# Silu on ScalarE in two of six blocks, weight pieces converted in pairs, and second-MoE units in paired buffers

## The chip, the cores and the metric

The kernel runs on one core of one Trainium2 chip. The metric is the device time of one execution in microseconds (us); lower is better. The core has five engines that run side by side, each through its own list of instructions in a fixed order: TensorE (PE, matmul), VectorE (DVE), ScalarE (ACT), GpSimd (POOL) and SyncE (SP), which issues the DMAs. An instruction that waits holds up all that stands behind it on its engine.

## The reference, cut to what matters

Three stages follow each other: a chunked linear attention (a scan with state), a gated MoE layer with Silu, and a second layer with a softmax-weighted activation and a layer norm.

```python
def reference(...):
    attn_out = _attn_ref(x, a, B, C)                 # 4 x 8 heads x 768 x 32, state 16, chunks of 32
    x = attn_out.transpose(0, 2, 1, 3).reshape(3072, 256)
    rms = np.sqrt(np.mean(x * x, axis=-1, keepdims=True) + 1e-06)
    xn = x / rms * rms_g                             # first MoE: 256 -> 1536 -> 256
    g = xn @ w_gate
    silu = g * (1.0 / (1.0 + np.exp(-g)))
    x = silu * (xn @ w_val) @ w_out
    h = x @ w_in                                     # second MoE: 256 -> 1024 -> 256
    e = np.exp(h - h.max(-1, keepdims=True))
    solu = h * (e / (e.sum(-1, keepdims=True) + 1e-09))
    mu, var = solu.mean(-1, keepdims=True), solu.var(-1, keepdims=True)
    return ((solu - mu) / np.sqrt(var + 1e-06) * g_ln) @ w_out2
```

## The kernel before

The 3072 tokens are 24 units of 128, and four units make a block (`BLOCKS`), so there are 6 blocks. For a unit, an attention step `y(u)` is made on PE from the decay matrix L (tile `L`, exponentials on ACT, mask on POOL), the products B by C (`cb`, tile `pcb`, turned into L by the two DVE operations `mt`), and the state (`s2`, `sbd`). The result is squared (`sq`), summed on PE (`ms`), raised to -0.5 on POOL (`ts`, `pw`), spread by a transpose (`rb`), multiplied in (`xc`, `xn`) and split into a high and a low float part (`xh`, `xl`). Every large product is made as three matmuls in fp32r: high by high, low by high, high by low.

For a block, the first MoE runs over 12 slices f of 128 hidden columns: gate `gm` into `pg` (6 matmuls of 128x512), value `vm` into `pv` (6), and, two slices later, the output `o` (6) into `po`. Between them stand `th` (ACT, tanh), `si` and `mu` (DVE, Silu and the product with the value), `ah` (ACT) and `al` (DVE or POOL), the split of the product. `pg` and `pv` have one PSUM bank each, so the next `gm` waits until the last reader of `pg` is done. The second MoE runs by unit: `h` into `ph`, maximum, `ex`, `so`, sums, `va`, two transposes `t` with split, `f` and the store.

The weights come as 64-bit numbers in 26 pieces of 512 KB. Each is loaded (`w_load`), turned into fp32 by three integer operations on DVE (`w_conv`, tile `wt`), and split by ACT (`wh`) and DVE or POOL (`w`).

No engine list is written by hand. `plan()` holds for every step its engine, a duration, a due time, what it comes after and which buffers it takes; it walks through time, picks on each engine the ready step with the earliest due time, and writes the steps out in that order. Constants at the top (`PRO`, `FIRST`, `Y0`, `HLAG`, `WGAP` and others) set the due times. Units 0 to 3 are made ahead of the first block (the prologue); the units of block b+1 are made during block b.

## Time and profile before

| | us |
|---|---|
| median of 3 runs (lowest to highest) | 565.83 (565.73 to 566.2) |
| the profiled execution, its own time | 565.08 |
| span of its profile | 563.4 |
| PE, DVE, ACT, POOL busy in the span | 546.5, 390.9, 290.3, 84.8 |
| mean granted TensorE clock | 0.981 of 2.4 GHz |

Times in a trace are us from the start of the span. The own time is 1.7 us above the span and 0.75 us below the median; a change of the span is taken one for one into the median. "Busy" of PE counts a pipelined matmul to its modelled end, so what a matmul costs in a row of them is the distance between starts.

### The profile page before, as it was taken

The page shows a single profiled execution, that of the slowest core. Times are in us where ns is not written, and L with a number is a line of the kernel's source. Part 1 is how long each engine was busy: PE and PEld are TensorE (multiplying, and loading weights), DVE is VectorE, ACT ScalarE, POOL GpSimd, SP SyncE. Part 2 cuts the span into 40 slices and gives each one's busy share as a digit, 9 for nine tenths or more (in the row PEclk, how much of TensorE's full clock was granted, in tenths as well). Part 3 has the DMA queues.
Part 4 walks back from the last instruction along what each step waited for, and adds up shares of the span by engine and source line. Part 5 has one row for each costly group of instructions (what it writes and reads, how often), then busy time and mean ns, then how long its engine had stood idle before and what let it go on. Part 6 is the DMA issues. An engine that isn't in the chain of part 4 may idle for free.

```text
span 563.4 us, 9443 instructions
## 1 busy us (share of the span) xinstructions
PE 546.5 (97%) x3544; PEld 461.1 (82%) x3544; DVE 390.9 (69%) x789; ACT 290.3 (52%) x654; POOL 84.8 (15%) x118
## 2 busy tenths in 40 slices
PE   9879998899999999999999999999999999999996
PEld 8757886687888888888888888888888888888795
DVE  5788999999876776575684574684674574564763
ACT  6437654666555564463474454554543353343464
POOL 2333323212221010110111100110100000000010
PEclk9579999999999999999999999999999999999999
DMA  7464765542022021121120220220200000000000
GB/s 213 132 212 140 216 203 194 182 145 71 14 72 76 2 80 47 43 72 36 54 76 11 75 70 10 80 70 10 72 2 9 10 1 9 11 1 10 9 20 30
DMA packets 44366, 39.33 MB, mean 70 GB/s; under 512 B 3936, under 2 KB 36896, under 8 KB 44320
## 3 DMA queue, kind: packets, MB, share of 16 engines
q1 hardware_dynamic: 44320, 38.72, 22.5%
q8 instruction: 28, 0.46, 0.4%
q14 instruction: 18, 0.15, 0.1%
HBM read 35.37 MB, written 3.34 MB: 69 GB/s over the span
## 4 chain that ended last, share of the span: by engine, by line
PE 81%; DVE 15%; DMA 2%; issue 1%; ACT 1%; SPq 0%; POOL 0%; DVEq 0%; ACTq 0%; POOLq 0%
PE pv L558 15%; PE pg L558 15%; PE po L600 14%; PE ph L436 12%; PE pf L538 12%; PE pt L514 4%; PE pcb L301 3%; DVE wt L119 2%; PE y L326 2%; DVE wt L122 2%; DVE th L580 2%; PE y L321 1%; DVE al L592 1%; DVE th L576 1%; DVE L L307 1%; DVE wt L116 1%
## 5 line engine op out<-in xcount | busy, mean ns | idle before, releaser
L586 ACT ACTIVATE ah<-th 128x512 fp32r<-128x512 f32 x72 | 45.2, 628 | 52.2 <-PE po L600 38.8
L580 DVE TENSOR_TENSOR th<-pv,th 128x512 f32<-128x512 f32 x72 | 49.8, 691 | 29.2 <-PE pv L558 24.1
L592 DVE TENSOR_TENSOR al<-th,ah 128x512 fp32r<-128x512 f32 x70 | 49.3, 704 | 26.0 <-ACT ah L586 25.6
L576 DVE SCALAR_TENSOR_TENSOR th<-th,pg 128x512 f32<-128x512 f32 x72 | 49.1, 682 | 20.0 <-ACT th L572 19.7
L558 PE MATMUL pg<-xh,wg_h 128*128 128x512 f32 x144 | 59.5, 413 | 2.3 <-ACT xh L401 1.2
L600 PE MATMUL po<-ah,wo_h 128*128 128x512 f32 x144 | 60.3, 419 | 0.0
L600 PE MATMUL po<-al,wo_h 128*128 128x512 f32 x144 | 56.7, 394 | 2.3 <-DVE al L592 2.3
L558 PE MATMUL pv<-xh,wv_h 128*128 128x512 f32 x144 | 58.4, 406 | 0.0
L558 PE MATMUL pg<-xh,wg_l 128*128 128x512 f32 x144 | 57.0, 396 | 0.0
L558 PE MATMUL pg<-xl,wg_h 128*128 128x512 f32 x144 | 56.8, 394 | 0.0
L600 PE MATMUL po<-ah,wo_l 128*128 128x512 f32 x144 | 56.7, 394 | 0.0
L558 PE MATMUL pv<-xl,wv_h 128*128 128x512 f32 x144 | 56.5, 392 | 0.0
L558 PE MATMUL pv<-xh,wv_l 128*128 128x512 f32 x144 | 56.4, 392 | 0.0
L572 ACT ACTIVATE th<-pg 128x512 f32<-128x512 f32 x72 | 42.6, 592 | 26.6 <-PE pg L558 26.4
L502 POOL TENSOR_TENSOR sc<-sc,mhalf 128x1 f32<-128x1 f32 x24 | 14.1, 587 | 263.6 <-DVE sc L497 263.6
L237 ACT ACTIVATE L<-L,cneg 128x128 f32<-128x128 f32 x160 | 50.5, 390 | 0.6 <-DMA L<-crow 0.6
L460 ACT ACTIVATE ut<-ph,sc 128x1024 f32<-128x1024 f32 x20 | 22.3, 1116 | 54.5 <-DVE sc L447 54.5
L538 PE MATMUL pf<-wo_h,uth 128*128 128x256 f32 x176 | 49.6, 282 | 0.3 <-DVE utl L528 0.2
L538 PE MATMUL pf<-wo_h,utl 128*128 128x256 f32 x176 | 49.6, 282 | 0.0
L538 PE MATMUL pf<-wo_l,uth 128*128 128x256 f32 x176 | 49.5, 281 | 0.0
L447 DVE TENSOR_REDUCE sc<-ph 128x1 f32<-128x1024 f32 x20 | 24.5, 1225 | 31.7 <-PE ph L436 31.7
L523 ACT ACTIVATE uth<-pt 128x512 fp32r<-128x512 f32 x44 | 26.0, 595 | 31.1 <-PE pt L514 30.9
(138 smaller groups left out, 1225.2 us busy)
## 6 DMA issues: line engine op xcount, KB each, us to landing
L<-crow SPq DMA_DIRECT2D x20, 512.0 KB
stage<-in_wo_dram SPq DMA_DIRECT2D x10, 512.0 KB
xb<-in_xbt_dram SPq DMA_DIRECT2D x24, 192.0 KB
stage<-in_wg_dram SPq DMA_DIRECT2D x6, 512.0 KB
bc<-in_bcT_dram SPq DMA_DIRECT2D x48, 64.0 KB
stage<-in_wv_dram SPq DMA_DIRECT2D x6, 512.0 KB
out_dram<-ob SPq DMA_DIRECT2D x24, 128.0 KB
stage<-in_wi_dram SPq DMA_DIRECT2D x4, 512.0 KB
```

The source lines that it names most:

```text
L237: A.activation(d["L"][:, h], d["L"][:, h], AF.Exp, bias=cneg[:, u * 8 + h:u * 8 + h + 1])
L436: T.matmul(ph[c], xx[:, kk, k * P:(k + 1) * P], ww[:, kk, 512 * c:512 * c + 512], start=(i == 0), stop=(i == 5))
L447: V.tensor_reduce(out=sc[:, 0:1], in_=ph[0], axis=AX.X, op=ALU.max, negate=True)
L523: A.activation(d["uT"][0][:, 4 * c:4 * c + 4].rearrange("p k t -> p (k t)"), d["ptc", c], AF.Copy)
L538: T.matmul(d["pf"][:, 0:DM], uu[:, k], ww[:, k], start=(k == 0 and i == 0), stop=(k == 7 and i == 2))
L558: T.matmul(ps[:, :n], ww[:, kk, f * P:(f + 1) * P], xx[:, kk, :n], start=(i == 0), stop=(i == 5))
L572: A.activation(d["th"], d["pg"], AF.Tanh, scale=0.5)
L576: V.scalar_tensor_tensor(out=d["th"], in0=d["th"], scalar=1.0, in1=d["pg"], op0=ALU.add, op1=ALU.mult)
L580: V.tensor_tensor(out=d["th"], in0=d["pv"], in1=d["th"], op=ALU.mult)
L586: A.activation(d["ah"], d["th"], AF.Copy)
L592: e.tensor_tensor(out=d["al"], in0=d["th"], in1=d["ah"].bitcast(F32), op=ALU.subtract)
L600: T.matmul(po[b, m][:, :n], ww[:, f, m * P:(m + 1) * P], aa, start=(f == 0 and i == 0), stop=(f == NF - 1 and i == 2))
```

## The change

1. **Silu in blocks 0 and 1** (`SILU = 2`). ACT computes Silu at once into `th`; `si` falls away, and `mu` becomes one `scalar_tensor_tensor` with a factor of 2 (blocks 2 to 5 keep tanh, `si` and `mu`). Silu and Exp are not in one table set, so ACT loads a table wherever it goes from one to the other: 20 loads in the program where there were 2.
2. **Weight pieces in pairs.** Two pieces share one staging tile, and the three integer operations run over 1024 elements, 13 times, where they ran over 512, 26 times. A conversion starts when both loads of the pair have landed. There are 2 paired staging buffers (4 single ones before) and 2 paired `wt` tiles (3 single ones before).
3. **Second-MoE units share buffers in pairs**: units 2k and 2k+1 have the two halves of one tile of tag `u`.
4. **The factor `rgt` moves from `xn` to `xc`**: `xc` is two ACT operations of 128 elements, `xn` one DVE operation of 256.
5. **Planner**: other due times, the identity matrix is loaded a few places later, `nid` is not made, a table switch is priced, and small matmuls (`warm`) are put into planned PE gaps of the prologue (5 of them come out).

```diff
-PRO = 34.0
-FIRST = 63.0
+PRO = 31.0
+FIRST = 70.0
...
-Y0 = (9.0, 4.0)
-YPOS, YSPAN = 0.65, 1.0
+Y0 = (8.0, 4.5)
+YPOS, YSPAN = 0.55, 0.92
...
-EARLY = (-1.0, 1.5, 4.0, 6.0)
+EARLY = (-5.0, 2.0, 6.0, 9.0)
...
-HLAG = (50.0, 26.0)
+WOFF = -4.0
+HLAG = (70.0, 10.0, 1)
...
+SILU = 2
+TABLE = 1.3
...
     def w_conv(i, c):
-        v = stg[i].rearrange("p (f w) -> p f w", w=2)
+        v = stg[i, 2].rearrange("p s (f w) -> p (s f) w", w=2)
         if c == 0:
-            wtm[i] = sp.tile([P, 512], I32, name="wt", tag="wt", bufs=BUFS["wt"])
-        t = wtm[i]
+            wtm[i, 2] = sp.tile([P, 1024], I32, name="wt", tag="wt", bufs=BUFS["wt"])
+            for q in range(2):
+                wtm[i + q] = wtm[i, 2][:, 512 * q:512 * q + 512]
+        t = wtm[i, 2]
...
     def at_xc(u):
...
-        A.activation(d["xts"], d["y"][:, 0:256].rearrange("p (g i) -> p g i", g=2), AF.Copy)
+        for g in range(2):
+            A.activation(d["xts"][:, g], d["y"][:, g * P:(g + 1) * P], AF.Copy, scale=rgt[:, g:g + 1])
...
     def at_xn(u):
...
-        for g in range(2):
-            V.scalar_tensor_tensor(out=d["xts"][:, g], in0=d["xts"][:, g], scalar=rgt[:, g:g + 1],
-                                   in1=d["y"][:, 384:512], op0=ALU.mult, op1=ALU.mult)
+        V.tensor_tensor(out=d["xts"], in0=d["xts"], in1=d["y"][:, 384:512].unsqueeze(1).to_broadcast([P, 2, P]), op=ALU.mult)
...
         if c == 0:
-            d["u"] = sp.tile([P, FF2], F32, name="ut", tag="u", bufs=BUFS["u"])
+            if u % 2 == 0:
+                upair[0] = sp.tile([P, 2, FF2], F32, name="ut", tag="u", bufs=BUFS["u"])
+            d["u"] = upair[0][:, u % 2]
...
-        A.activation(d["th"], d["pg"], AF.Tanh, scale=0.5)
+        if b < SILU:
+            A.activation(d["th"], d["pg"], AF.Silu)
+        else:
+            A.activation(d["th"], d["pg"], AF.Tanh, scale=0.5)
...
-        V.tensor_tensor(out=d["th"], in0=d["pv"], in1=d["th"], op=ALU.mult)
+        if b < SILU:
+            V.scalar_tensor_tensor(out=d["th"], in0=d["th"], scalar=2.0, in1=d["pv"], op0=ALU.mult, op1=ALU.mult)
+        else:
+            V.tensor_tensor(out=d["th"], in0=d["pv"], in1=d["th"], op=ALU.mult)
...
+    def warm(u, n):
+        if u not in st:
+            return
+        for _ in range(n):
+            T.matmul(st[u]["y"][:, 322:384], ones, ones[:, 0:62], start=True, stop=True, skip_group_check=True)
...
+            if e == "ACT" and o.get("tab", table[0]) != table[0]:
+                t += TABLE
```

**PE in the prologue.** From the first `y` (rows `y<-L,xb` and `y<-xb`; `y<-cd` is its part with the state) to the second. `pcb` is `cb`, `y<-ones,sq` is `ms`, `pg` and `pv` from `um,la` are the exponents of L for a later unit, `y<-ident,r` is `rb`. Before:

```order
L301 MATMUL pcb<-bc 128x128 x8
L326 MATMUL y<-L,xb 32x128 x8
L331 MATMUL y<-xb 32x64 x4
L259 MATMUL pg<-um,la 128x128 x4
L361 MATMUL y<-ones,sq 128x1 x2
L259 MATMUL pv<-um,la 128x128 x4
L321 MATMUL y<-cd,sbd 128x128 x2
```

With the change:

```order
L338 MATMUL y<-L,xb 32x128 x8
L343 MATMUL y<-xb 32x64 x4
L313 MATMUL pcb<-bc 128x128 x8
L373 MATMUL y<-ones,sq 128x1 x2
L271 MATMUL pg<-um,la 128x128 x4
L271 MATMUL pv<-um,la 128x128 x4
L395 MATMUL y<-ident,r 128x128
L333 MATMUL y<-cd,sbd 128x128 x2
```

The `cb` of unit 1 now stands behind the first `y`, and the `ms` of unit 0 stands ahead of both groups of exponents instead of between them.

**DVE at the start of block 0.** The last conversions of the prologue and the first slices of the MoE (`th<-th,pg` is `si`, `th<-pv,th` or `th<-th,pv` is `mu`, `al` the low part). Before:

```order
L394 SCALAR_TENSOR_TENSOR xts<-xts,rgt,y 128x128 x2
L133 TENSOR_TENSOR wv_l<-wt,wv_h 128x2x256
L405 TENSOR_TENSOR xl<-xts,xh 128x2x128
L122 SCALAR_TENSOR_TENSOR wt<-stage,wt 128x512
L116 TENSOR_SCALAR wt<-stage 128x512
L119 SCALAR_TENSOR_TENSOR wt<-stage,wt 128x512
L133 TENSOR_TENSOR wo_l<-wt,wo_h 128x512
L122 SCALAR_TENSOR_TENSOR wt<-stage,wt 128x512
L576 SCALAR_TENSOR_TENSOR th<-th,pg 128x512
L580 TENSOR_TENSOR th<-pv,th 128x512
```

With the change, from the second half of the last `y` of the prologue on:

```order
L416 TENSOR_TENSOR xl<-xts,xh 128x2x128
L354 SCALAR_TENSOR_TENSOR s_461<-s_390,e_170,y 128x64
L360 TENSOR_TENSOR sbd<-cst,s_461 128x256
L386 TENSOR_SCALAR r<-y 128x1
L134 SCALAR_TENSOR_TENSOR wt<-stage,wt 128x1024
L406 TENSOR_TENSOR xts<-xts,y 128x256
L128 TENSOR_SCALAR wt<-stage 128x1024
L416 TENSOR_TENSOR xl<-xts,xh 128x2x128
L131 SCALAR_TENSOR_TENSOR wt<-stage,wt 128x1024
L145 TENSOR_TENSOR wo_l<-wt,wo_h 128x512
L145 TENSOR_TENSOR wg_l<-wt,wg_h 128x2x256
L134 SCALAR_TENSOR_TENSOR wt<-stage,wt 128x1024
```

The conversions are half as many and twice as long, and the last `xn` of the prologue (`xts`) stands behind one of 1024 elements.

**ACT in block 0.** From the second Tanh or Silu on (`th`); `L` with `x8` or `x4` are the exponentials of a unit of the next block, `w.._h` is the high part of a weight piece. Before:

```order
L572 ACTIVATE th<-pg 128x512
L237 ACTIVATE L<-L,cneg 128x128 x8
L246 ACTIVATE e_515<-e_515 128x128
L586 ACTIVATE ah<-th 128x512
L572 ACTIVATE th<-pg 128x512
L129 ACTIVATE wv_h<-wt 128x2x256
L237 ACTIVATE L<-L,cneg 128x128 x8
L586 ACTIVATE ah<-th 128x512
```

With the change:

```order
L587 ACTIVATE th<-pg 128x512
L141 ACTIVATE wv_h<-wt 128x2x256
L141 ACTIVATE wo_h<-wt 128x512
L606 ACTIVATE ah<-th 128x512
L587 ACTIVATE th<-pg 128x512
L249 ACT_TABLE_LOAD
L249 ACTIVATE L<-L,cneg 128x128 x8
L258 ACTIVATE e_494<-e_494 128x128
L606 ACTIVATE ah<-th 128x512
L249 ACTIVATE L<-L,cneg 128x128 x4
L141 ACTIVATE wg_h<-wt 128x2x256
```

The exponentials are one slice later, with a table load ahead of them; another load follows them, before the next Silu.

## Rows read from the trace of the kernel before

**Rows 1.** The page, busy time by engine (share of the span, instructions).

```profile
PE 546.5 (97%) x3544; PEld 461.1 (82%) x3544; DVE 390.9 (69%) x789; ACT 290.3 (52%) x654; POOL 84.8 (15%) x118
```

**Rows 2.** Windows: stretch, its length, busy time of each engine, granted clock, DMA, GB/s.

```profile
1.00:40.20 39.20, 33.11 (x286) 29.73 (x286) 26.97 (x65) 19.26 (x54) 13.27 (x18) 0.79 0.63 182
40.20:43.80 3.60, 3.58 (x8) 2.76 (x9) 3.26 (x7) 1.22 (x3) 0.00 (x0) 0.50 1.10 340
43.80:126.60 82.80, 79.38 (x520) 63.45 (x519) 80.17 (x150) 51.41 (x129) 24.60 (x28) 1.00 0.56 178
126.60:140.00 13.40, 12.43 (x88) 9.56 (x87) 12.95 (x23) 8.63 (x21) 3.13 (x4) 1.00 0.26 75
140.00:524.10 384.10, 384.10 (x2414) 325.03 (x2412) 244.37 (x482) 188.45 (x406) 40.63 (x60) 1.00 0.13 38
524.10:563.36 39.26, 33.93 (x233) 30.53 (x232) 23.22 (x67) 21.13 (x46) 2.75 (x5) 0.99 0.06 21
```

**Rows 3.** Timeline of PE in the prologue: start, duration, what, idle before.

```profile
11.76 1.16 PE L301 MATMUL pcb<-bc 16*128 16x128 f32 x16
12.85 0.64 PE L326 MATMUL y<-L,xb 128*32 128x128 f32 x16
...
13.54 1.16 PE L259 MATMUL pg<-um,la 128*128 128x128 f32 x8
...
16.64 1.01 PE L361 MATMUL y<-ones,sq 128*128 128x1 f32 x4 [1.95 <-DVE s L340]
...
19.36 1.06 PE L321 MATMUL y<-cd,sbd 128*128 128x128 f32 x4
...
28.42 1.06 PE L321 MATMUL y<-cd,sbd 128*128 128x128 f32 x4
...
33.23 0.61 PE L321 MATMUL y<-cd,sbd 128*128 128x128 f32 x4
...
40.22 0.79 PE L558 MATMUL pg<-xh,wg_h 128*128 128x512 f32 x1 [1.21 <-ACT xh L401]
```

**Rows 4.** Windows, PE alone: stretch, length, busy, granted clock, DMA, GB/s.

```profile
16.00:17.00 1.00, 0.36 (x2) 0.82 0.67 120
...
18.00:30.00 12.00, 12.00 (x89) 0.50 0.28 88
```

**Rows 5.** Groups of DVE by line: form, count, busy, mean ns, idle before; 43.8 to 126.6.

```profile
L119 DVE SCALAR_TENSOR_TENSOR wt<-stage,wt 128x512 int32<-128x512 int32 x16 | 12.0, 753 | 0.1
L122 DVE SCALAR_TENSOR_TENSOR wt<-stage,wt 128x512 int32<-128x512 int32 x16 | 11.9, 745 | 0.3
...
L576 DVE SCALAR_TENSOR_TENSOR th<-th,pg 128x512 f32<-128x512 f32 x16 | 10.9, 681 | 0.6 <-ACT th L572 0.6
...
L116 DVE TENSOR_SCALAR wt<-stage 128x512 int32<-128x512 int32 x17 | 7.9, 466 | 0.0
...
L394 DVE SCALAR_TENSOR_TENSOR xts<-xts,rgt,y 128x128 f32<-128x128 f32 x10 | 3.0, 341 | 0.0
```

**Rows 6.** Groups by line over the whole span, the nearest forms to the new operations.

```profile
L470 DVE SCALAR_TENSOR_TENSOR ut<-ph,ut 128x1024 f32<-128x1024 f32 x20 | 24.5, 1224 | 20.3 <-ACT ut L460 20.3
...
L405 DVE TENSOR_TENSOR xl<-xts,xh 128x256 fp32r<-128x256 f32 x24 | 10.4, 435 | 2.9 <-ACT xh L401 2.8
```

**Rows 7.** Timeline of ACT, the second of the two table loads.

```profile
5.53 1.28 ACT L267 ACT_TABLE_LOAD   x1 [2.06 <-DVE cneg L1026]
6.83 1.14 ACT L267 ACTIVATE L<-pg,cneg 128x128 f32<-128x128 f32 x4
```

**Rows 8.** Timeline of PE, 92 to 141, the rows with idle time before them.

```profile
95.75 0.50 PE L600 MATMUL po<-al,wo_h 128*128 128x512 f32 x1 [1.84 <-DVE al L592]
...
106.72 0.50 PE L600 MATMUL po<-al,wo_h 128*128 128x512 f32 x1 [0.49 <-DVE al L592]
...
111.87 0.50 PE L558 MATMUL pg<-xh,wg_h 128*128 128x512 f32 x1 [0.98 <-DVE th L576]
...
139.64 0.32 PE L383 MATMUL y<-ident,r 128*128 128x128 f32 x1 [0.78 <-POOL r L379]
```

More of the change, by code (lines that the diff above doesn't have):

```diff
@@ L407, in at_xl @@
         st.pop(u)
+    upair = [None]
     x2 = {}
@@ L799, in m_f4 @@
             m_f(u, c)
-    win = [f"{p}{i}" for i in range(18, 22) for p in ("wh", "w")] + ["wc25.2"]
+    win = [f"{p}{i}" for i in range(18, 22) for p in ("wh", "w")] + ["wc12.2"]
     wout = ["plo0", "plo1"]
@@ L901, in fused_kernel, with ld_ident, c_nid @@
     op("wd", "ACT", 0.35, 5.5, (c_wdec,), after=["sf"], use=["pd"])
+    def ld_ident():
+        S.dma_start(ident, consts[:, 3 * P:4 * P])
+    def c_nid():
+        V.tensor_scalar(out=nid, in0=ident, scalar1=-1.0, scalar2=None, op0=ALU.mult)
+    op("idn", "SP", 0.45, 4, (ld_ident,), kb=64)
+    if VIA_PE:
+        op("nid", "DVE", 0.25, 6, (c_nid,), after=["idn"])
+        for i in VIA_PE:
+            ops[f"wp{i}"]["after"].append("nid")
+    ops["rb0"]["after"].append("idn")
     op("cst", "SP", 0.9, 5, (ld_cst,), kb=128)
@@ L905, in fused_kernel @@
         ops[f"sbd{u}"]["after"].append("cst")
-        ops[f"xn{u}"]["after"].append("cst")
+        ops[f"xc{u}"]["after"].append("cst")
     early = [f"lpe{u}.{g}" for u in range(NPE) for g in range(2)] + ["e1p"] + ["cr0", "cr1"]
     ops["wh22"]["after"] += early + ["sf"]
+    def warm(u, n):
[3 more added lines that the diff above has]
+            T.matmul(st[u]["y"][:, 322:384], ones, ones[:, 0:62], start=True, stop=True, skip_group_check=True)
+    for nm, o in ops.items():
+        if o["e"] == "ACT" and nm[:2] in ("lx", "e1", "ex", "wd"):
+            o["tab"] = "exp"
     def plan():
         users = {}
+        table = ["exp"]
         for o in ops.values():
@@ L958, in est, with mg @@
             return t
-        while len(order) < len(ops):
+        def mg(nm, e):
+            if nm[0] == "w" and nm[1] != "d":
+                return WMG
+            return MARGIN.get(e, 0.0) if free[e] > PRO else 0.0
+        lasty = None
+        while len(end) < len(ops):
             best = None
@@ L985, in plan @@
                 ready[e].remove(nm)
+            if nm[0] == "y":
+                lasty = int(nm[1:])
+            if e == "PE" and lasty is not None and t < PRO + 6 and t - free[e] > 0.5:
+                order.append((free[e], (warm, lasty, int((t - free[e]) * FILL / 0.22))))
             order.append((t, nm))
+            if e == "ACT":
+                table[0] = o.get("tab", table[0])
             if e == "SP":
                 free[e] = t + o["us"]
-                dma_free = max(dma_free, t + 1.3) + o["kb"] / 300.0
+                dma_free = max(dma_free, t + 1.3) + o["kb"] / DRATE
                 end[nm] = dma_free + 1.0
```

67 lines of the change are left out of this document (37 added, 30 removed).

## The prediction

> **What bounds the kernel now.** I read the page's busy times first, then windows over the span, then PE's timeline where the windows show it short of work. PE is busy 97% of the span [rows 1], and from 140.0 to 524.1 it is busy without a break, 384.10 of 384.10, at a granted clock of 1.00 [rows 2]. The change leaves PE's products as they are, so those 384 us can't shrink; time can only come from three other stretches. The prologue to 40.2 has a mean clock of 0.79 and 33.1 us busy out of 39.2. The stretch from 43.8 to 126.6, block 0 and half of block 1, has DVE busy 80.2 of 82.8 and PE 79.4: there DVE is the bound, by a little. The tail behind 524.1 has PE busy 33.9 of 39.3 [rows 2].
>
> Inside the prologue PE stands idle 1.95 us ahead of the first `ms`, which waits for work behind DVE's state copy; then the granted clock falls from 1.00 to 0.50 and stays there for the 12 us from 18 to 30 although PE is busy in all of them [rows 3, 4]. 0.50 is 1.2 GHz, the lower of the two levels. What that costs is seen between the `y` of successive units: 12.85, 19.36, 28.42, 33.23 and then the first gate matmul at 40.22 [rows 3]. Gate matmuls run at half clock again until 43.8 [rows 2].
>
> **The change, term by term.** The sum is made against the profiled execution's own 565.08 us (span 563.4 and 1.7 around it).
>
> *Term A, the first gate matmul comes earlier.* In the new order the `cb` of unit 1 stands behind the first `y` instead of ahead of it, so that `y` starts 11.76 to 12.85 = 1.09 us earlier, at about 11.75 [rows 3]. After it PE has `cb` (1.09) and then `ms`, and no exponents stand ahead of `ms`: the 1.95 us of idle time has other PE work in it, since ACT's squares need that long anyway while `cb` runs. From the first `y` to the second PE has `y` 0.69 (12.85 to 13.54), `cb` 1.09, `ms` about 0.5 (half of the 1.01 at half clock), two groups of exponents at 1.16 or less, and the transpose, some 0.3: 4.6 to 4.9 us at full clock [rows 3]. I take 4.6, so 16.35. Second to third `y`: 9.06 us before, at half clock [rows 3, 4], of which half would be 4.5; DVE has a paired conversion in it now, and I take 5.0, so 21.35. Third to fourth: 4.81 before, its first two us at half clock [rows 3]; I take 4.4, so 25.75. Fourth `y` to gate: 6.99 before [rows 3], and DVE's list is what it follows. There the new list has one `tensor_scalar` and two `scalar_tensor_tensor` of 1024 elements where the old one had two and three of 512. A `scalar_tensor_tensor` of 1024 took 1.22 in another step, one of 512 took 0.75 here, a `tensor_scalar` 0.47 [rows 5, 6]: 1024 elements of the latter lie between 0.47 and 0.93, and I take 0.75. New 0.75 + 2 x 1.22 = 3.2, old 2 x 0.47 + 3 x 0.75 = 3.2: nothing. `xn` is one operation of 256 elements, 0.44 as the split of that size, for two of 0.34 [rows 5, 6]: 0.24 less each, 0.5 for the two that stand there. So 6.5, and the gate comes at 32.3 instead of 40.2: **-7.9**. Bounds: with 5.7 for the last step, 31.5 (-8.7); with the clock falling where it fell before, the second to third `y` takes its 9.06 again and the gate comes at 36.4 (-3.8). The matmuls called `warm` fill a fraction of PE's last gap; I take it that the clock still falls ahead of the gate and the first matmuls are as slow as before. If it doesn't, 3.6 us at half clock [rows 2] become 1.8, -1.8 more.
>
> *Term B, block 0 and half of block 1.* PE's gaps there are 1.84, 0.49 and 0.98, and 0.78 more at 139.6, 4.1 us together; all but the last are behind DVE [rows 8]. DVE's load in 43.8 to 126.6 changes so: 16 `si` of 0.68 go, -10.9 [rows 5]. Conversions: 16 pieces took 12.0 + 11.9 + 7.9 = 31.8 [rows 5]; ten pairs stand in the same stretch of the new order, 10 x (0.75 + 2 x 1.22) = 31.9, so nothing for 4 more pieces. The `w` splits on DVE go from 10 to 17, since the planner gives POOL fewer, at the 0.68 of `si`, which also reads two tensors of 512: +4.8. `xn` gives 5 x 0.24 = -1.2. Together 80.2 - 7.3 = 72.9, against 79.5 that PE needs there (82.8 less its gaps of 3.3): 92% instead of 97%. ACT's load grows: 51.4 [rows 2], plus ten table loads of 1.28 [rows 7], plus 3.3 as my allowance for the doubled `xc` and four more `wh`: 67.5, or 85%. `si` read `pg` last; now `th` does, which frees the bank earlier. Two engines near 90% that wait for each other still leave some gaps, so I take 2.3 of the 4.1: **-2.3**; bounds -4.1 and 0.
>
> *Term C, the tail.* The `f` of the unit ahead of the last block stands ahead of the tail's `h` products now, so its softmax no longer shares DVE and ACT with theirs. PE idles 39.3 - 33.9 = 5.4 us from there to the end, some 3.7 of them the last store [rows 2]. I take **-0.5**, bounds 0 and -1.0.
>
> *Costed at nothing.* The other eight table loads lie in the rest of block 1, where ACT is busy 8.6 of 13.4 us and then 188 of 384 [rows 2], 10 us more in about 60. The paired `u` tiles hold a buffer until the second unit is done; PE has other work queued for many us at that place, and with that gone it would cost about one softmax chain, 5 us, once. The loads: the second piece's first operation already waits for nothing but DVE's own list, and the queue reaches that load at the same place in its list, so waiting for a pair costs nothing in the prologue; behind it, DMA is busy 0.56 of block 0 [rows 2].
>
> Sum: 565.08 - 7.9 - 2.3 - 0.5 = 554.4. The median stands 0.75 above the profiled execution, so **555.1**.
>
> **The rivals.**
>
> *The clock falls early again (chance 0.17).* If a wait that I don't see leaves PE idle near 16 us, the prologue runs at half clock as it did: A is -3.8, the time 555.1 + 4.1 = 559.2. For it: the clock fell after one gap of 1.95 and took until 30 to come back [rows 3, 4]. Against it: by the walk PE has work back to back from the first `y` to the fourth.
>
> *ACT becomes the bound (0.12).* The load row shows 2.06 us of idle time ahead of it, put down to DVE [rows 7]. If that were the switch's own, a switch would take up to 3.34. ACT needs 54.7 without its ten loads; it reaches PE's 79.5 at 2.48 per switch, and at 3.0 it needs 84.7: B is lost and 5.2 added, 555.1 + 7.5 = 562.6. Against it: the Exp behind the load starts at 6.83, 0.02 after its end, and the wait has an owner. The Trainium skill, "ScalarE: Activation LUTs", section "What ACT_TABLE_LOAD costs", puts a switch at 1283 ns for the load and 1380 ns for a drain; the row agrees on the first and shows no drain behind the load. By that 2.66 ACT would need 81.3, by estimate 1.8 over PE, and the time would be near 559.
>
> *Slower: the switches stand in the chain (0.06).* `th` waits for `gm`, `mu` for `th`, `ah` for `mu`, `al` for `ah`, and `o` on PE for `al`; behind the third Silu two loads and eight exponentials stand ahead of the next Silu. Each of the 18 added loads that PE can't cover costs 1.28 [rows 7], all of them 23.0, which makes 555.1 + 23 = 578. My gain of 10.7 is used up from 8 to 9 exposed loads on. Against it: a load ahead of a Silu has no wait of its own and runs while `gm` does, and PE has `vm` and `o` of two slices back between two `gm`.
>
> *It does not do what it says (0.03):* conversions of a pair take as long as two, DVE stays at 97%, and the prologue keeps its order of waits in another place: near 565.
>
> **How the numbers follow.** My forecast, gate near 32 and no new wait of weight, has 0.62 and gives 552 to 558. The range takes in the early clock fall and half of the ACT case at the top, 561; at the bottom all bounds at once are 565.08 - 8.7 - 1.8 - 4.1 - 1.0 + 0.75 = 550.2, and I go to 550.5. Faster by over 0.2% (1.1 us, about what a measurement of this kernel can tell): 0.62 + 0.17 + 0.11 = 0.90; within it 0.04; slower 0.06.
>
> **What would show it.** A: the first gate matmul at 31.5 to 33 in PE's timeline, a granted clock of 1.00 from 14 to 28, successive `y` 4.4 to 5.0 apart. B: from the first Silu to the fifth of block 1 DVE busy 92% or less, ACT about 85%, PE's gaps 2 us together; table loads of 1.28 each, mostly inside ACT's idle time. C: PE idle behind the last `o` of block 5 by half a us less. I am wrong if the clock is 0.50 in the prologue again, if `ah` behind a table load releases PE's waits, or if the conversions of 1024 take over 1.5.

## The result, and the profile after

The changed kernel takes 569.04 us (median of 6 runs, 566.85 to 570.2) against 565.44 for the kernel before on the same chip (6 runs, 561.95 to 566.2): a ratio of 1.0093, 95% interval 1.0065 to 1.0122. It is slower; 555.1 was predicted. The profiled execution took 568.03 (span 566.1). One kernel's executions differ by several us (3.4 and 4.3 in these six and six), and the mean granted clock goes with them: before, from 561.2 us at 0.993 to 566.35 at 0.981 over all its runs here.

The page's busy times after, which answer to [rows 1]: PE has the same work and ten small `warm` matmuls; DVE has 18.8 us less, ACT 31.4 more.

```profile
PE 546.4 (97%) x3554; PEld 459.5 (81%) x3554; DVE 372.1 (66%) x716; ACT 321.7 (57%) x696; POOL 76.5 (14%) x103
```

Windows after, cut at the first gate matmul, the first Silu and the fifth Silu of block 1 (the cuts at 43.8 and 126.6 in [rows 2] lie 0.6 behind and 0.8 ahead of the same Tanh). 524.1 is the same time as in [rows 2], not the same event; from 140 to it PE has no gap in either kernel. The last row goes from the first gate matmul of block 0 to that of block 1, and the fence under it has the same row of before.

```profile
1.00:35.40 34.40, 29.05 (x296) 26.22 (x296) 21.18 (x48) 18.26 (x56) 12.03 (x17) 0.90 0.63 184
35.40:38.40 3.00, 2.99 (x7) 2.33 (x8) 3.00 (x6) 2.32 (x3) 0.00 (x0) 0.50 1.07 357
38.40:127.40 89.00, 83.69 (x525) 65.35 (x525) 77.10 (x119) 65.28 (x140) 17.90 (x18) 0.98 0.55 176
...
524.10:566.09 41.99, 33.97 (x213) 29.87 (x211) 21.96 (x65) 19.41 (x42) 2.74 (x5) 0.96 0.05 17
35.41:106.87 71.46, 66.32 (x410) 51.48 (x411) 61.91 (x95) 53.94 (x115) 13.86 (x14) 0.95 0.61 191
```

```profile
40.20:107.98 67.78, 65.32 (x416) 52.07 (x417) 65.34 (x122) 40.22 (x100) 20.05 (x22) 0.97 0.60 190
```

Three stretches make up the difference of the two spans. To the first gate matmul: 40.22 to 35.41, -4.8. From there to the first gate matmul of block 1: 67.76 to 71.46, +3.7. From there to the end: 455.4 to 459.2, +3.8. Together +2.7, as 563.4 to 566.1. So the prologue gave less than forecast, and block 0 and what follows took where they were to give.

**The prologue.** PE's timeline after, against [rows 3], and PE's clock in four windows, against [rows 4].

```profile
10.86 0.68 PE L338 MATMUL y<-L,xb 128*32 128x128 f32 x16
...
13.92 0.61 PE L373 MATMUL y<-ones,sq 128*128 128x1 f32 x4 [1.19 <-ACT xts L402]
...
17.83 0.78 PE L333 MATMUL y<-cd,sbd 128*128 128x128 f32 x4
...
23.08 0.61 PE L333 MATMUL y<-cd,sbd 128*128 128x128 f32 x4
...
28.03 0.61 PE L333 MATMUL y<-cd,sbd 128*128 128x128 f32 x4
...
30.35 0.66 PE L952 MATMUL y<-ones 128*128 128x62 f32 x4 [1.02 <-ACT xts L402]
...
32.37 1.54 PE L952 MATMUL y<-ones 128*128 128x62 f32 x6 [0.97 <-DVE r L386]
...
35.41 0.80 PE L572 MATMUL pg<-xh,wg_h 128*128 128x512 f32 x1 [1.02 <-ACT xh L412]
```

```profile
14.00:18.00 4.00, 4.00 (x22) 0.60 0.57 187
18.00:28.00 10.00, 8.89 (x119) 0.99 0.46 137
100.00:103.40 3.40, 3.40 (x11) 0.52 0.58 190
550.00:554.00 4.00, 3.83 (x20) 0.58 0.00 0
```

The wait ahead of the first `ms` is 1.19 us where it was 1.95; the clock still falls, to 0.60 over 4 us (1.6 us lost) instead of 0.50 over 12 us (6.0). The clock's part, 4.4, is most of the 4.8.

**Block 0.** PE's rows with idle time before them, from 57 to 107: five, 5.1 us, where before had two (1.84 and 0.49, [rows 8]). The clock falls behind the fourth (0.52 from 100.0 to 103.4), 1.6 us more.

```profile
68.31 0.51 PE L620 MATMUL po<-al,wo_h 128*128 128x512 f32 x1 [1.43 <-DVE al L612]
79.39 0.50 PE L572 MATMUL pg<-xh,wg_h 128*128 128x512 f32 x1 [1.23 <-ACT wg_h L141]
87.24 0.61 PE L373 MATMUL y<-ones,sq 128*128 128x1 f32 x4 [0.49 <-DVE s L352]
99.77 0.74 PE L373 MATMUL y<-ones,sq 128*128 128x1 f32 x4 [1.45 <-ACT xts L402]
106.87 0.49 PE L572 MATMUL pg<-xh,wg_h 128*128 128x512 f32 x1 [0.54 <-ACT xh L412]
```

The first is behind conversions: `ah` was done at 64.66, but `al` stood on DVE behind two steps of 1.2 us and started at 67.57. What stood ahead of the fourth, in ACT's timeline: `sq` is behind a load and a Silu, though its `y` had long been written.

```profile
95.95 0.61 ACT L141 ACTIVATE wo_h<-wt 128x512 fp32r<-128x512 f32 x1
96.58 1.28 ACT L587 ACT_TABLE_LOAD   x1
97.87 0.60 ACT L587 ACTIVATE th<-pg 128x512 f32<-128x512 f32 x1
98.36 0.38 ACT L367 ACTIVATE sq<-y 128x256 f32<-128x256 f32 x1
```

**The end.** From 524.1 on PE idles 8.0 us (41.99 - 33.97) where it idled 5.3 [rows 2], and the clock is 0.58 from 550 to 554, 1.7 more. Between block 0 and the end PE gained: before has gaps of 0.98 and 0.78 there [rows 8] and a small one, 2.0 us in all, and 0.2 are left.

**Prices.** The new operations cost about what was assumed (a `tensor_scalar` of 1024 0.685 for 0.75, a `scalar_tensor_tensor` 1.22), and the loads what [rows 7] showed. These are groups of the whole span after.

```profile
L131 DVE SCALAR_TENSOR_TENSOR wt<-stage,wt 128x1024 int32<-128x1024 int32 x13 | 15.9, 1222 | 0.2
...
L128 DVE TENSOR_SCALAR wt<-stage 128x1024 int32<-128x1024 int32 x13 | 8.9, 685 | 0.0
```

```profile
L587 ACT ACT_TABLE_LOAD x9 | 11.5, 1283 | 0.1
L249 ACT ACT_TABLE_LOAD x8 | 10.3, 1283 | 0.1
```

### The profile page after: what moved, and what is told of

Its sections match the earlier page's. It is cut to its first block, busy times and chain, and to the rows that moved or that the text cites. A ratio compares the mean times of both kernels' runs of the same rounds, so it can differ in the third digit from the quotient of the medians.

```text
span 566.1 us, 9384 instructions
## 1 busy us (share of the span) xinstructions
PE 546.4 (97%) x3554; PEld 459.5 (81%) x3554; DVE 372.1 (66%) x716; ACT 321.7 (57%) x696; POOL 76.5 (14%) x103
## 4 chain that ended last, share of the span: by engine, by line
PE 83%; ACT 7%; DVE 6%; DMA 2%; issue 1%; SPq 0%; ACTq 0%; DVEq 0%
PE pg L572 16%; PE pv L572 15%; PE po L620 15%; PE pf L552 13%; PE ph L448 11%; PE pcb L313 3%; PE pt L528 3%; PE y L338 2%; ACT L L249 2%; DMA cd<-in_bcT_dram 1%; PE y L333 1%; DVE wt L134 1%; PE y L373 1%; ACT L587 1%; ACT L249 1%
## 5 line engine op out<-in xcount | busy, mean ns | idle before, releaser
L612 DVE TENSOR_TENSOR al<-th,ah 128x512 fp32r<-128x512 f32 x65 | 47.0, 723 | 27.7 <-ACT ah L606 26.2
L572 PE MATMUL pg<-xh,wg_h 128*128 128x512 f32 x144 | 60.7, 421 | 2.8 <-ACT xh L412 1.6
L474 ACT ACTIVATE ut<-ph,sc 128x1024 f32<-128x1024 f32 x20 | 22.3, 1115 | 39.1 <-DVE sc L459 39.1
L593 DVE SCALAR_TENSOR_TENSOR th<-th,pg 128x512 f32<-128x512 f32 x48 | 32.8, 683 | 14.7 <-ACT th L589 13.9
L557 ACT ACTIVATE ob<-pf,sc 128x256 f32<-128x256 f32 x24 | 11.4, 473 | 53.0 <-PE pf L552 33.3
L391 POOL TENSOR_TENSOR r<-r,mhalf 128x1 f32<-128x1 f32 x24 | 15.5, 644 | 183.9 <-DVE r L386 167.5
L589 ACT ACTIVATE th<-pg 128x512 f32<-128x512 f32 x48 | 28.5, 594 | 18.7 <-PE pg L572 18.6
L448 PE MATMUL ph<-wi_h,xh 128*128 128x512 f32 x96 | 38.2, 398 | 0.0
```

Of the source, the lines that this page charges most:

```text
L448: T.matmul(ph[c], xx[:, kk, k * P:(k + 1) * P], ww[:, kk, 512 * c:512 * c + 512], start=(i == 0), stop=(i == 5))
L474: A.activation(d["u"], ph[0], AF.Exp, bias=sc[:, 0:1], accum_out=sc[:, 1:2])
L572: T.matmul(ps[:, :n], ww[:, kk, f * P:(f + 1) * P], xx[:, kk, :n], start=(i == 0), stop=(i == 5))
L589: A.activation(d["th"], d["pg"], AF.Tanh, scale=0.5)
L593: V.scalar_tensor_tensor(out=d["th"], in0=d["th"], scalar=1.0, in1=d["pg"], op0=ALU.add, op1=ALU.mult)
L612: e.tensor_tensor(out=d["al"], in0=d["th"], in1=d["ah"].bitcast(F32), op=ALU.subtract)
```

## The experiments

The table has, for each kernel, the ratio to the kernel before (on the same chip, with its interval), and of its profiled execution the first gate matmul, the stretch from it to the first gate matmul of block 1, PE's idle time in that stretch (gaps over 0.1 us), and the rest. All but the ratio come from one execution each. What block 0 has beyond its idle time is in good part PE at a lower clock: the mean granted clock in it is 0.97 in before, 0.95 in the changed kernel, 0.93 in e4, 0.92 in e5 and e12, 0.90 in e1 and 0.89 in e8.

| kernel | ratio | first gate | block 0 | idle in it | rest |
|---|---|---|---|---|---|
| before | 1 | 40.22 | 67.8 | 2.4 | 455.4 |
| changed | 1.0093 [1.0065, 1.0122] | 35.41 | 71.5 | 5.1 | 459.2 |
| e1 tanh in place | 1.0092 [1.0055, 1.0129] | 35.77 | 72.4 | 3.0 | 459.3 |
| e2 old lags | 1.0074 [1.0045, 1.0104] | 38.64 | 71.4 | 4.7 | 457.7 |
| e3 single pieces | 1.0124 [1.0096, 1.0152] | 36.80 | 71.4 | 5.1 | 459.8 |
| e4 no Silu | 1.0212 [1.0179, 1.0244] | 36.25 | 75.9 | 6.9 | 461.4 |
| e5 Silu alone | 1.0132 [1.0096, 1.0168] | 36.72 | 77.1 | 9.1 | 454.9 |
| e6 pairs alone | 1.0045 [1.0019, 1.0071] | 38.03 | 68.0 | 3.2 | 457.7 |
| e7 all numbers of before | 1.0178 [1.0141, 1.0216] | 38.83 | 74.7 | 6.9 | 460.9 |
| e8 block numbers of before | 1.0182 [1.0140, 1.0223] | 37.60 | 76.1 | 5.2 | 459.8 |
| e9 nine moves | 1.0129 [1.0099, 1.0158] | 37.56 | 70.4 | 5.0 | 461.4 |
| e10 e5 with tanh | 1.0098 [1.0068, 1.0129] | 38.44 | 75.1 | 8.5 | 454.6 |
| e11 e5, earlier units | 1.0079 [1.0052, 1.0106] | 41.01 | 71.5 | 4.5 | 457.1 |
| e12 prologue alone | 1.0238 [1.0210, 1.0266] | 38.75 | 77.4 | 7.8 | 459.8 |
| e13 moves in before | 0.9994 [0.9971, 1.0018] | 36.85 | 67.8 | 2.4 | 455.7 |
| e14 short conversions | 1.0043 [1.0024, 1.0061] | 37.23 | 69.2 | 4.2 | 459.2 |
| e15 short and tanh | 0.9913 [0.9882, 0.9943] | 35.92 | 64.0 | 0.4 | 457.1 |
| e16 four moves in before | 1.0028 [1.0007, 1.0049] | 38.76 | 67.7 | 2.4 | 455.8 |
| e17 and three in block 0 | 1.0021 [1.0001, 1.0041] | 38.19 | 68.5 | 1.7 | 456.7 |
| e18 single, old lags | 1.0088 [1.0062, 1.0115] | 39.38 | 71.3 | 5.1 | 457.2 |

### Are the table loads the cause?

**e1**, the changed order without the loads:

```
-            A.activation(d["th"], d["pg"], AF.Silu)
+            A.activation(d["th"], d["pg"], AF.Tanh)
```

> The changed kernel in its own order, with Tanh in place of Silu in blocks 0 and 1: the value of the activation is left out (a plain tanh stands there), every instruction keeps its place, and the 18 added table loads are gone, since Tanh and Exp share a table. Theory 'loads in the chain': in block 0 the xh, sq and wg_h behind a load release PE's waits, so the lead of 5.6 us that the prologue gives is kept instead of lost between 58 and 108 us; time 569.0 - 5 = 564, the gaps of 1.23 (at 77.8), 1.45 (97.9) and 0.54 (105.9) gone, and the clock drop behind the 1.45 too. Rival 'conversions of 1024': what makes al and the state copy late is DVE's list (1.43 at 66.5, 0.49 at 86.4); the gaps stay or move, time within 1.5 us of 569.

Measured: 1.0092, no better than with the loads. The waits for ACT shrank as expected (for `wg_h` from 1.23 to 0.16, for the scaled copy from 1.45 to 0.26), but that for `al` grew from 1.43 to 2.11, and behind it the clock fell to 0.56 for 11 us, 4.8 us lost:

```profile
69.36 0.50 PE L620 MATMUL po<-al,wo_h 128*128 128x512 f32 x1 [2.11 <-DVE al L612]
```

```profile
66.00:69.00 3.00, 1.24 (x6) 1.00 0.06 23
69.00:80.00 11.00, 10.64 (x55) 0.56 0.51 150
```

The theory "loads in the chain" fell as the sole cause. Of six executions one had a mean clock of 0.988 and took 564.85, the other five, at 0.975 to 0.982, 569.2 to 571.6. The longer wait came with the loads' going: the exponentials ended earlier, so POOL's select of `L` started ahead of this `al` and not behind it, and the `al` took 0.90 us longer (last section).

### Which part of the change costs?

**e3**, single pieces in the changed kernel (core of the edit; single tiles for the `u` units too, four `u` buffers and three `wt`), and **e4**, no Silu:

```
-        for k in range(0 if i % 2 else 3):
-            op(f"wc{i//2}.{k}", "DVE", 0.69 if k == 0 else 1.22, ...
+        for k in range(3):
+            op(f"wc{i}.{k}", "DVE", 0.41 if k == 0 else 0.68, ...
```

```
-SILU = 2
+SILU = 0
```

> The changed kernel with single pieces: weights are loaded and converted one piece of 512 at a time through four buffers, and every second-layer unit has its own buffer, as before; Silu, the planner's other numbers and the prologue are those of the change, and the planner makes its order anew. Theory 'loads in the chain' plus 'cover moved out of the tail': neither has to do with the pairs, so 568 to 570, with gaps of the same size in block 0 behind ACT. Rival 'conversions of 1024': al and the state copy no longer stand behind 2.4 us of conversion, PE's gaps in block 0 fall from 5.8 to under 3, and the time is 565 to 566.

> The changed kernel with Silu in no block (tanh and the product on DVE again in blocks 0 and 1), planned anew; pairs, prologue and lags are those of the change. Theory 'loads in the chain': no added load, but DVE has 16 more operations of 0.68 from 43 to 127 us and is the bound again, at about 97%: block 0 loses some 2 us to it, less than to the loads; 565 to 567. Rival 'conversions of 1024': DVE is fuller and coarser than before, so the gaps grow: 570 or more.

Measured: 1.0124 and 1.0212. Neither part taken out of the changed kernel makes it faster. As the planner made a new order for each, this doesn't price the parts; it shows that taking one out doesn't bring the loss back. e3, at 570.59 us, came near what the first theory said, with 5.1 us of idle time in block 0, and "conversions of 1024" fell as the sole cause; e4, at 575.45, is as bad as that rival wanted, and PE's longest wait in its block 0 (2.32, for a scaled copy of ACT) bears it out: the copy itself waited 2.28 us for DVE's state copy, which stood behind two conversion steps, one of them lengthened to 2.17 beside an `al` of POOL. The next (1.92) is for a split of DVE that took 1.36 beside POOL's select.

```profile
80.89 2.17 DVE L134 SCALAR_TENSOR_TENSOR wt<-stage,wt 128x1024 int32<-128x1024 int32 x1
...
83.22 0.62 ACT L402 ACTIVATE xts<-y,rgt 128x128 f32<-128x128 f32 x2 [2.28 <-DVE s L352]
```

**e5** and **e6**, one part put into the kernel before; e5 adds the lines of the change on Silu with `SILU = 2` and `TABLE = 1.3`, e6 those on pairs:

```
+        if b < SILU:
+            A.activation(d["th"], d["pg"], AF.Silu)
```

```
-            d["u"] = sp.tile([P, FF2], F32, name="ut", tag="u", bufs=BUFS["u"])
+            if u % 2 == 0:
+                upair[0] = sp.tile([P, 2, FF2], F32, name="ut", tag="u", bufs=BUFS["u"])
+            d["u"] = upair[0][:, u % 2]
```

> The kernel before with one part of the change: Silu on ScalarE in blocks 0 and 1 (and the planner's price for a table load), no si on DVE there; pieces, prologue and all numbers are those of before, and the order of PE's tail is too. Theory 'numbers': Silu by itself relieves DVE, which is the bound between 43.8 and 126.6; the run without Silu was 6.4 us above the changed kernel, so Silu is worth 3 to 5 us here too: 560 to 562, with PE's gaps of [rows 8] behind DVE gone. Rival 'loads in the chain': the 18 loads put the xh, sq and w splits late, PE gets gaps behind ACT of 1 to 1.5 us each, 565 to 568.

> The kernel before with another part of the change alone: pieces loaded and converted in pairs of 1024 elements, second-layer units in paired buffers; tanh, prologue and numbers of before. Its tail order differs from before in the last two units (all 16 transposes of the last unit in one go ahead of its 48 products). Theory 'numbers': pairs are no loss in block 0 (the run with single pieces was 1.5 us above the changed kernel), and the tail costs 1 to 2: 564 to 567. Rival 'conversions of 1024': PE waits in block 0 for al and state copies that stand behind 2.4 us of conversion, 569 or more.

Measured: pairs alone 1.0045 (as the theory "numbers" said, block 0 is no longer, 68.0, and the rest is 2.3 longer), Silu alone 1.0132, against the theory "numbers". In e5 PE idles 6.1 us close together, in three gaps ahead of block 1 (below).

**e7** and **e8**, the changed kernel with numbers of before:

```
-FIRST = 70.0
+FIRST = 63.0
-HLAG = (70.0, 10.0, 1)
+HLAG = (50.0, 26.0, 1)
```

(and in both YPOS, YSPAN, WGAP and WMG, in e7 also PRO, Y0, SLACK0, EARLY, CROW and DRATE.)

> The changed kernel with every number of the planner's table set back (PRO, FIRST, Y0, YPOS, YSPAN, SLACK0, EARLY, CROW, WGAP, HLAG, the margin and the DMA rate): Silu, pairs, the scaled copies on ACT and the later load of the identity matrix stay. Theory 'numbers': the time that block 0 loses is set by the order that these numbers make, so 561 to 564, with the tail's gap of 2.5 of the paired buffers still there. Rival 'the operations themselves' (loads and pairs): 567 to 570 as with the new numbers.

> The changed kernel with five of the numbers set back, those that act behind the prologue (FIRST 63, YPOS and YSPAN 0.65 and 1.0, WGAP 8, HLAG 50 and 26, the margin of weight steps 0); the prologue's numbers stay. Theory 'numbers': the first gate matmul comes at 35.4 to 36 and block 0, paced for 63 and not for 70 us, keeps more of that lead: 561 to 564. Rival 'the operations themselves': the lead of 5 us is lost by 108 us again, 567 to 570.

Measured: 1.0178 and 1.0182. The theory "numbers" fell: with the changed operations the old numbers are worse than the new ones.

**e12**, the change's prologue without Silu and pairs (the edit of e3 and e4, with the numbers of e8):

> The kernel before with the prologue of the change (PRO, Y0, EARLY, SLACK0, CROW, the DMA rate, the scaled copies on ACT, the later load of the identity matrix, the fill matmuls), without Silu and without pairs, and with the block numbers and the tail order of before. If term A is right, the first gate matmul comes near 35.5 to 37 and the rest is as before: 561 to 562 on a chip where before takes 563 to 565. If the prologue's gain is only what the clock gives or takes by chance (the kernel of Silu alone has the old prologue and reached 36.7), no difference from before can be measured.

Measured: 1.0238, the slowest of all, where 561 to 562 us were expected, though its DVE has about the work of before (393.0 us). Block 0 was made anew by the planner and takes 77.4; the gate at 38.75 gave nothing that can be seen behind that.

### Loads or order, in the kernel of Silu alone

**e10** (e5 with Tanh for Silu, as e1) and **e11**:

```
-YPOS, YSPAN = 0.65, 1.0
+YPOS, YSPAN = 0.55, 0.92
```

> The kernel of Silu alone (numbers of before) in its own order with Tanh in place of Silu, so without the 18 table loads; the activation's value is left out. Theory 'order of waits': the stall of 3.7, 1.0 and 1.4 us at the start of block 1 stays, since the norm chain of the last unit has no products of PE beside it and its state copy stands behind three conversion steps on DVE: 568 to 570. Rival 'loads in the chain': the stall is gone and the time is 561 to 563.

> The kernel of Silu alone with YPOS and YSPAN of the change (0.55, 0.92 for 0.65, 1.0): the units of the next block are due earlier, the rest as there. Theory 'order of waits': the norm chain of the last unit of block 1 lies beside products of block 0 again and the stall of 6 us and its half clock at the start of block 1 go: 560 to 564. Rival 'loads in the chain': the time stays at 568 to 571, with gaps behind ACT elsewhere.

Measured: 1.0098 and 1.0079. PE's timeline of e10, with no load anywhere near, ahead of block 1:

```profile
104.55 1.16 PE L303 MATMUL pcb<-bc 16*128 16x128 f32 x16
109.61 1.01 PE L363 MATMUL y<-ones,sq 128*128 128x1 f32 x4 [3.90 <-ACT xts L391]
111.64 0.47 PE L385 MATMUL y<-ident,r 128*128 128x128 f32 x1 [1.02 <-POOL r L381]
113.50 0.80 PE L560 MATMUL pg<-xh,wg_h 128*128 128x512 f32 x1 [1.39 <-ACT xh L403]
```

The stall of e5 (3.71, 1.02, 1.39) is here as long (3.90, 1.02, 1.39), with a lowered clock (0.64 from 110 to 120), so the loads don't make it. What is left is the order: in it the last unit's norm chain has no products of block 0 beside it, and DVE is busy 5.40 of the 5.50 us from 104.5 to 110. Units that are due earlier (e11) take 5.6 us off block 0, and the stall there falls to 2.37 and 1.21, but the 560 to 564 us expected of it were missed (569.19, the time that the rival gave). Its profiled execution was the slowest of eight, with the latest first gate of all, 41.01.

### Can the five gaps be moved away?

**e9**, nine steps of the finished order moved ahead of what stood before them:

```
+        MOVES = (("al0.5", "wc5.1"), ("wh12", "xh5"), ("wh13", "xh5"), ("lx7.0", "lx7.1"), ("s26", "wc7.2"),
+                 ("sq7", "th0.10"), ("xc7", "th0.10"), ("xh7", "lx9.0"), ("xl7", "wc9.2"))
```

> The changed kernel with nine steps of the finished order moved by hand within block 0, none added or taken away: each of PE's five gaps there (66.5, 77.8, 86.4, 97.9, 105.9 us in the trace after) has its releaser put ahead of the work that stood before it: al 0.5 ahead of the conversion steps of a pair, wh12 and wh13 ahead of xh5, the exponentials of unit 7 (with their load) behind them, the state copy of unit 6 ahead of a conversion step, sq and xc of unit 7 ahead of a Silu and its load, xh and xl of unit 7 ahead of a load with four exponentials and of a conversion step. Theory 'order of waits' (what PE waits for stands behind other work in its engine's list; load shares don't tell it): PE's gaps of 5.3 us there fall to under 2, the clock fall at 100 us (1.7) goes, and the time is 4 to 6 less than the changed kernel's: 563 to 565, with the tail as late as before. Rival 'ACT and DVE are simply full' (the work is late wherever it stands): the gaps come back a few us later, 567 to 569.

Measured: 1.0129. The five gaps went and others came: 5.1 us of idle time in block 0 again (70.44 - 65.30 by PE's window), and 2.15 more for a Silu at 115.0, in block 1. My theory that five places in the lists make the loss fell; the rival held, that the work is late wherever it stands.

### Is it DVE, ACT, or both?

**e14**, the changed order with most of each conversion left out, and **e15**, that with Tanh for Silu as well:

```
-            V.scalar_tensor_tensor(out=t, in0=v[:, :, 1], scalar=-0x40000000, in1=t, ...
+            V.scalar_tensor_tensor(out=t[:, :128], in0=v[:, :128, 1], scalar=-0x40000000, in1=t[:, :128], ...
```

> The changed kernel in its own order with the two scalar_tensor_tensor steps of each conversion on 128 of 1024 elements; the rest of the weights' exponents and low bits is left out. DVE has some 2 us less per pair, 14 to 16 us less in block 0. Rival 'DVE is still the bound of block 0, by its latency': PE's gaps there go, the lead of 5.6 us is kept to 108 us and beyond, 563 to 564 with the late tail. Theory 'order of waits between ACT, DVE and PE': only the gaps behind al and the state copy (1.43, 0.49) go, those behind ACT (1.23, 1.45, 0.54) stay: 566 to 568.

> As the run with short conversions, and Tanh in place of Silu too, so that ACT has no added loads; both the activation's value and most of the conversion are left out, the order is that of the changed kernel. If DVE and ACT together hold PE in block 0, all its gaps there go now and the first gate matmul of block 1 comes near 101 (35.4 + 66): 561 to 563 with the late tail. If gaps of more than 2 us stay, the order of PE's own list or the units' norm chains hold it.

Measured: 1.0043 and 0.9913, that is 566.74 and 558.55 us. The windows of block 0 (first gate to first gate) and PE's waits in it (in all, times, longest), e14 first:

```profile
37.23:106.43 69.20, 65.02 (x411) 50.94 (x411) 47.12 (x96) 54.02 (x115) 12.00 (x14) 0.96 0.61 193
```

```profile
PE y L373 <- ACT xts L402: 2.2, 2, 1.5
PE pg L572 <- ACT xh L412: 1.8, 2, 1.0
PE pg L572 <- ACT wg_h L141: 1.2, 1, 1.2
```

```profile
35.92:99.97 64.05, 63.68 (x411) 51.27 (x411) 47.11 (x96) 40.90 (x105) 12.26 (x14) 0.97 0.64 201
```

With DVE at 68% every wait left is for ACT: 1.45 and 1.22 us are those for the scaled copy and `wg_h` that stand behind a load in the changed order (one of the two for `xh`, 1.0, is that ahead of the first gate itself). Without the loads too (DVE 74%, ACT 64%) 0.4 us is left and block 0 takes 64.0. So ACT's loads and DVE's conversions hold PE together: against the changed kernel's 1.0093, the loads alone taken away (e1) give nothing, the conversions alone 0.5% (2.8 us), both 1.8% (10 us). Up to block 1 PE's, DVE's and ACT's lists are the same in e1, e14, e15 and the changed kernel but for the loads, so it is one order: its idle time in block 0 is 5.1 us as it stands, 3.0 without the loads, 4.2 with short conversions, 0.4 with both.

### The tail

**e2**, the old lags, and **e18**, the edit of e3 with the old lags too:

```
-HLAG = (70.0, 10.0, 1)
+HLAG = (50.0, 26.0, 1)
```

> The changed kernel with the old lag numbers of the second layer, HLAG = (50, 26) for (70, 10): the order of PE's last products is again that of the kernel before, with the products of units 18 and 19 between those of the last block. Theory 'cover moved out of the tail': PE's gaps of 2.03 and 0.98 in the tail go, the tail is 4 us shorter, 569.0 - 4 = 565. Rival 'the tail is late for another reason' (DVE's backlog, the paired u buffers): the gaps stay, 568 to 569.

> The run with single pieces and single second-layer buffers, now with the old lags (50, 26) too: the tail's order is that of before, word for word. If the tail's loss follows the lags and the paired buffers and nothing else, the last 20 us lose nothing against before (the run with single pieces lost 2.7 there, the run with old lags and pairs 2.9); block 0 stays as late as with single pieces: 567 to 569.

Measured: 1.0074 and 1.0088. From the start of the last `o` product to the end of the span, the kernels with old lags and single buffers (before, e5, e10 to e13, e16 to e18) take 39.1 to 39.5; those with old lags and pairs 41.9 (e2, e6), and 43.3 and 44.5 (e8, e7). PE's row in e2 that makes it, a gap that before doesn't have:

```profile
554.97 2.40 PE L528 MATMUL pt<-ident,ut 128*128 128x128 f32 x9 [2.53 <-DVE ut L488]
```

With the new lags the gap is another one, the same with pairs (the changed kernel) and with single buffers (e3):

```profile
550.17 0.36 PE L552 MATMUL pf<-wo_h,xh 128*128 128x256 f32 x1 [2.03 <-DVE xl L542]
```

```profile
553.77 0.36 PE L546 MATMUL pf<-wo_h,xh 128*128 128x256 f32 x1 [2.03 <-DVE xl L536]
```

So each of the two edits costs the tail some 2.5 us by itself (pairs 41.9 - 39.5, a fall of the clock behind the gap with it; lags by the last column, e3 to e18, 459.8 - 457.2), and they don't add: with both, one gap stands in place of the other. e18 is as late as e3 in block 0, as expected.

### The prologue and its clock

**e13**, the kernel before with three steps of unit 0 moved, **e16**, one more, and **e17**, three in block 0 as well (`al0.9` ahead of `xl6`, `al0.11` ahead of `xn7`, `si1.0` ahead of `x2l0.1`):

```
+        MOVES = (("y0", "wc1.2"), ("s20", "wc1.2"), ("sq0", "wh1"), ("xc0", "wh1"))   # e13
+        MOVES += (("lpe2.1", "ms0"),)                                                 # e16
```

(y0 itself only changes its place against DVE's steps, not on PE.)

> The kernel before, its order kept but for three steps of the prologue: the state copy, the squares and the scaled copy of unit 0 stand ahead of the last conversion step of the second piece (DVE) and of that piece's split (ACT), so that the first ms no longer waits 1.95 us [rows 3]. Theory 'a gap of 2 us lowers the clock and the order made anew loses what that gives': the clock doesn't fall near 16 us, or for less, the first gate matmul comes at 36 to 37, and block 0, whose order is untouched, keeps the gain: 560.5 to 562.5 where before takes 563 to 565. Rival 'block 0 eats any lead' (DVE is its bound, so an earlier gate is waited away): the gate is earlier but the first gate matmul of block 1 stays at 108, and the time is within 0.5 us of before.

> The kernel of the three moves in before with one more: the second exponent group of unit 2 on PE stands ahead of the first ms, so that PE has work where it still waited 1.24 us. Theory 'a gap in the prologue lowers the clock': no gap over 1 us is left near 15 us, the clock doesn't fall there, the first gate matmul comes near 36 in nearly every execution, and the time is that of before's best executions, 561 to 562 against a median of before of 563.7. Rival 'the fall comes by chance of the execution, not by this gap': the times still spread from 561.5 to 566 and the median is not below that of before by more than the measurement tells.

> The same kernel with three moves in block 0 and at the start of block 1 as well: al of slice 9 ahead of a unit's xl, al of slice 11 ahead of the unit's xn, and si of the first slice of block 1 ahead of half the split of the second layer's input, each of them the releaser of a gap of PE in before (1.84, 0.49, 0.98 us, [rows 8]). If these gaps are a matter of order alone, 2 us less than the run with four moves; if DVE as the bound gives them back a slice later, as the changed kernel did with its nine moves, no less or up to 3 us more.

PE's rows and clock in e13:

```profile
16.00 0.61 PE L361 MATMUL y<-ones,sq 128*128 128x1 f32 x4 [1.24 <-ACT xts L389]
...
36.85 0.79 PE L558 MATMUL pg<-xh,wg_h 128*128 128x512 f32 x1 [1.21 <-ACT xh L401]
```

```profile
16.00:21.00 5.00, 5.00 (x45) 0.66 0.40 125
```

and in e16:

```profile
15.50 0.60 PE L361 MATMUL y<-ones,sq 128*128 128x1 f32 x4 [0.16 <-ACT xts L389]
17.69 0.71 PE L321 MATMUL y<-cd,sbd 128*128 128x128 f32 x4 [1.59 <-DVE sbd L348]
```

```profile
18.00:29.00 11.00, 11.00 (x96) 0.53 0.32 95
```

In e13's profiled execution the gate came 3.4 us earlier and block 0 and the rest kept it (67.8 and 455.7): with an order left as it is, a lead survives. But over twelve runs the ratio is 0.9994, no difference: the kernel before has executions as good (561.35 the best of 23 here, 561.48 the best of e13). In e16 the work put into the first gap moved a gap of 1.59 us to the second `y`, the clock fell there, and all twelve executions had 0.981 to 0.984; it is 0.28% slower, and the 561 to 562 us expected were missed. In e17 before's own gaps in block 0 fall from 2.4 to 1.7 us, and the next one, at the start of block 1, grows from 0.98 to 1.39: no gain. Of the kernels that leave nothing out, none is faster than before by more than its interval.

## Why the prediction was wrong

**Term A (-7.9): right in kind, too large, and in part not the change's.** Its sum took `y` 4.6, 5.0 and 4.4 apart and 6.5 to the gate; they were 6.97, 5.25, 4.95 and 7.38, from a first `y` at 10.86, 0.9 earlier than it took. The step that failed is the first of the four, 2.4 us over: the sum has "PE has work back to back", but ACT's squares and copies were later than `cb` covered, PE idled 1.19 us, and the clock fell behind that. The last of the four has three waits of about 1 us along the norm chain. The larger fault is the base: the 6 us at half clock of [rows 4] are a matter of the execution. With the prologue of before (DVE's and ACT's lists up to the gate are the same), four profiled executions have the first gate at 40.22, 36.72, 38.44 and 41.01 (mean 39.1; before, e5, e10, e11), and the clock from 18 to 30 is 0.50, 0.86, 0.57 and 0.50 in them; with the prologue after, five have 35.41, 35.77, 38.64, 36.25 and 37.56 (mean 36.7; after, e1, e2, e4, e9). By these means the change is worth 2.4 there, not 7.9. With four and five executions that lie 4.3 and 3.2 us apart this is an estimate; by it half of the 4.8 is luck of the two profiled executions.

**Term B (-2.3): the sign was wrong, and this step failed most.** The shares came out below the forecast: from first to fifth Silu DVE is busy 87% (77.10 of 89.00; 92% forecast) and ACT 73% (65.28; 85% forecast). But they did so because the stretch grew: in us DVE has 77.1 where 72.9 were forecast, between cuts 1.4 us wider, and ACT 65.3 where 67.5 were. The step that failed is "two engines near 90% that wait for each other still leave some gaps, so I take 2.3 of the 4.1": a load share was turned into idle time. Before has DVE at 96% in block 0 and 2.4 us of PE's idle time; the changed kernel has 87% and 5.1. PE's gaps are not lack of time on one engine. They are places where a chain of alternating steps on ACT and DVE arrives late (one was ready behind other work on DVE, another on ACT), and e14 and e15 show both engines in them at once. The loads do hold PE, but only a part of the gaps goes when they alone go. And wherever operations or numbers were changed, the planner made the order anew: the eleven kernels so planned have 3.2 to 9.1 us of idle time in block 0 (changed, e2 to e8, e11, e12, e18; nine different orders of it, since e2 has that of the changed kernel and e18 that of e3), never before's 2.4. The least, pairs alone, costs block 0 0.2 us. That an order with Silu and few gaps can't exist isn't shown; none was found here. Behind block 0 the term held: 2.0 us of gaps became 0.2.

**Term C (-0.5): the sign was wrong.** The step that failed is that the `f` of the unit ahead of the last block, moved forward, leaves DVE and ACT freer for the tail. But its products on PE were the cover for the tail's chains: e3 and e18 differ in the lags alone, and the gap of 2.03 is there with the new ones only. PE idles 2.7 us more there than in before, and a clock fall adds 1.7.

**What was costed at nothing.** Loads: some 7 of the 10 us that e15 gives come from taking them away, but only once the conversions are short. Paired `u` tiles: "PE has other work queued for many us at that place" was false for the last unit, where pairs with the old lags make a wait of 2.53 (e2). Pair conversions at no cost held for pairs alone (block 0 at 68.0), but not in the changed order, where `al` and a state copy stand behind them and PE waits 1.43 and 0.49.

**The rivals.** *The clock falls early* came in a shorter form, and its price for term A, -3.8, is near the -4.8 measured. *ACT becomes the bound* by a drain didn't: the load at 96.58 starts 0.02 behind the end of the step before it, and the Silu 0.01 behind the load's. The Trainium skill, "ScalarE: Activation LUTs", section "What ACT_TABLE_LOAD costs", gives 1283 ns for the load, and these rows agree to the nanosecond; of the 1380 ns of drain that it adds they show nothing. *The switches stand in the chain* is nearest to what happened, at a chance of 0.06; it counted exposed loads at 1.28 each and had no term for the order, the tail or the clock. What the runs point to, a new order with more waits in it, was no rival at all. Which part of the change made this order worse than before's isn't shown, and order alone doesn't decide: the same order has 0.4 us of idle time in block 0 once loads and conversions are light.

## What to carry to other kernels

A busy share says which engine can't take more work; it doesn't say how long another engine waits for it, and relief on one of two engines that alternate in a chain may give nothing until the other is relieved too, so count the gaps and their owners, and take each owner away in a kernel of its own. Where a planner orders the work, a change of operations or numbers can be a new order, whose waits can be worth more than the change: price that with both signs, and read the order at the places where the old one had cover, at block borders and in the tail. And before a gain is taken from a stretch at half clock, look at several executions: it may not be there in most of them.
